# A router's constants moved into a planned instruction list, with other estimates for clears, and five deferred operations moved ahead of a loop

## The chip, the core and the metric

The kernel runs on one core of a Trainium2 chip. The metric is device time in microseconds (us) of one execution; the time shown is a median of runs. TensorE (PE) multiplies matrices, VectorE (DVE) and ScalarE (ACT) work elementwise, GpSimd (POOL) makes indices and issues indirect DMAs, and SyncE (SP) issues the other DMAs. Each engine works through its own instructions in order and waits for others at semaphores.

## What is computed

A recurrence over 768 steps for 32 heads of width 40, then a mixture of experts with one expert for each of 3072 tokens, then a dense MLP:

```python
for t in range(S):                                    # recurrence
    y[:, :, t] = np.einsum('bhd,bhde->bhe', rt, state)
    Sa = np.einsum('bhde,bhe->bhd', state, at)
    state = state * wt[:, :, None, :] - np.einsum('bhd,bhe->bhde', Sa, bt) \
            + np.einsum('bhd,bhe->bhde', vt, kt)
x = y.transpose(0, 2, 1, 3).reshape(3072, 320)
logits = x @ w_gate + modality_bias[modality_id]      # router, 8 experts
e_idx = np.argmax(logits, axis=1)
gate_w = softmax(logits)[np.arange(N), e_idx]
for e in range(8):                                    # first MLP: 320 -> 1024 -> 320
    out[mask] = gate_w[mask, None] * (np.maximum(x[mask] @ w1[e], 0.0) @ w2[e])
h = out @ w_in                                        # second MLP: 320 -> 2048 -> 320
return (h * (1.0 / (1.0 + np.exp(-1.702 * h)))) @ w_out
```

## The kernel before

Operands of matmuls are split into two fp16 parts, high and low, whose products are added in PSUM.

**The recurrence** (class Attn) goes in 24 chunks of 32 steps. Work that doesn't depend on the state is done ahead: the decays (clamped on DVE, then two scans and transposes), the triangular solves, the products of keys and values. The state S is carried from chunk to chunk in two halves (the DVE instruction "S<-s,P", 46 of them). After each chunk a row of 128 tokens goes through the router: `row` scales and splits it, PE multiplies by the gate, and for groups of up to four chunks `route` picks the expert and scatters the tokens to DRAM (POOL's indirect DMAs "XD<-XR,desti"). Near the end the first experts' weights are fetched ("raw<-in_W,w0row") and the first slots of the first MLP are computed.

All of this is written down as a list of operations (class Plan), not issued at once. `emit` estimates the length of each operation (`cost`), runs nine rounds of a forward and a backward list schedule over the engines, and issues the instructions in the order of the best round; on the chip each engine then takes them in that order. Some operations may go to either of two engines (`either`, with the engine chosen by the planner): the clears of large zeroed tiles (`clear`: gbd, tbd, nbd, xbd, zbd, kb, pick), the roundings of masked products (mg), the placings of blocks in the zeroed tiles (gbd, tbd, xbd, zbd), and others. In the profile nearly all of this has line L250, which is that of the issuing helper.

The router's constants (identity and triangle masks, index tables made by POOL's iota and cast on DVE, gate weights split in two parts, the bias by modality) are made by `consts`, ahead of the list and outside it, in program order. Their temporaries have a pool of their own. In the list a clear on DVE is estimated by

```python
if op == "memset":
    return 10 + n * (0.85 if eng == "gpsimd" else 0.26 if half else 1.04)
```

**The first MLP** (`moe1`) goes through slots of 128 tokens in order of experts. Beside it the weights of the second MLP are loaded as 64-bit numbers, put together from words on DVE (tiles wt and f, lines L1113 to L1119) and split (OH on ACT, OL on DVE, lines L1141 and L1142). What is left of that at the end is a generator, `self.rest`, whose pieces are taken one at a time by `next(self.rest, None)`: four at the end of `moe1`, then one in each round of the second MLP's loop but the round k = 1.

**The second MLP** (`moe2`) runs through 96 steps, each a block of 512 tokens by 128 hidden columns: `up` on PE, `gate` (t on DVE, sigmoid on ACT), `high` (g on DVE, gh on ACT), `low` (gl on DVE), and three steps later `down` (acc on PE). In this part a scheduler of the framework keeps nearly the order of the program.

Of the kernel before, what the change touches and what calls it, by code (L numbers as in the profile page):

```python
# [14 lines left out]
class Pool:  # L15


    def __init__(self, pool, bufs):
        self.pool, self.bufs, self.tiles, self.turn = pool, bufs, {}, {}
# [26 lines left out]
class Given:  # L46
# [5 lines left out]
    def tile(self, shape, dt, tag=None, name=None):  # L52
        ts = self.tiles[tag or name]
        ts.append(ts.pop(0))
        assert list(ts[-1].shape) == list(shape) and ts[-1].dtype == dt, tag
        return ts[-1]


class Carve:
# [23 lines left out]
class Plan:  # L83
# [117 lines left out]
    def cost(self, eng, op, a, k):  # L201
        aps = [p for x in list(a) + list(k.values()) for p in self.aps(x)]
        out = k["out"] if "out" in k else a[0]
        n = max(self.size(p) for p in aps)
        psum = any("PSUM" in str(getattr(p.tensor, "_space", "")) for p in aps)
        half = all(p.dtype == mybir.dt.float16 for p in aps if self.size(p) > 1)
        if eng == "tensor":
            m = self.size(out)
            wide = k["lhsT"].dtype != mybir.dt.float16 if op == "matmul" else True
            return max(m * (2 if wide else 1) / PEHZ + (2.5 if PEHZ > 2 else 0), 20.0 if op == "matmul" and self.size(k["lhsT"]) <= 32 else 25.0)  # L210
        if eng == "scalar":
            return ((51 if psum else 93) + n / 1.2 + (190 if "accum_out" in k else 0)
                    + (94 if isinstance(k.get("scale"), bass.AP) else 0))
        if op == "indirect_dma_start":
            return 1040.0
        if op == "memset":
            return 10 + n * (0.85 if eng == "gpsimd" else 0.26 if half else 1.04)
        if op == "affine_select":
            return 130 + n
        if eng == "gpsimd":  # L220
            return 147 + (1.888 if out.dtype == mybir.dt.float16 else 2.1) * n
        if eng == "sync":
            if op == "dma_start":
                return 475.0 if k["out"].ap[0][1] == 128 else 650.0
            return 1180.0 if n <= 512 else 1245.0 if n <= 1024 else 2140.0
        if op == "reciprocal":
            return 69 + 6.2 * n
        if op == "tensor_tensor_scan":
            return 2.13 * n
        if op == "transpose":  # L230
            return 1.9 * n
        if op == "tensor_tensor" and max(len(p.ap) for p in aps) > 4:
            return 69 + 1.75 * n
        rate = 1.0
        if op == "tensor_copy" and not psum:
            rate = 0.25 if half else 0.5
        elif op == "tensor_scalar" and not psum:
            rate = 0.35 if half else 0.5
        return 69 + n / 0.96 * rate
# [276 lines left out]
class Mlp:  # L516
# [4 lines left out]

    def consts(self, w_gate, modality, bias):
        tc, ctx = self.tc, self.ctx
        p = self.cp = ctx.enter_context(tc.tile_pool(name="mconst", bufs=1))
        with tc.tile_pool(name="mtemp", bufs=1) as tp:
            self.consts_in(p, tp, w_gate, modality, bias)

    def consts_in(self, p, tp, w_gate, modality, bias):
        nc = self.nc
        self.id16 = p.tile([128, 128], F16, name="id16")  # L530
        self.idb = p.tile([128, 128], mybir.dt.bfloat16, name="idb")
# [45 lines left out]
        m = tp.tile([128, NTILE], mybir.dt.int64, name="mod")  # L577
# [392 lines left out]
    def next(self, xp):  # L970

        self.xtile = lambda: xp.tile([128, XROW], F32, tag="xg", name="xg")

    def moe1(self, fill, flags):
# [3 lines left out]
        with tc.tile_pool(name="m1", bufs=2, side="right", reuse_waits="tile") as p, \  # L978
# [81 lines left out]
            self.rest = fill[2]()  # L1060
            fill[0](NFIX - 1)
            down(NFIX - 1, to=last)
            for _ in range(4):
                next(self.rest, None)

    def slots(self, fit, p, ps):

# [197 lines left out]
    def moe2(self, out):  # L1265
# [5 lines left out]
        with ExitStack() as c2, \  # L1271
# [47 lines left out]
            def done(b, c):  # L1319
# [6 lines left out]
                if b == NB - 1:  # L1326
# [4 lines left out]
                sent.append(nc.gpsimd.indirect_dma_start(  # L1331
                    out=out, out_offset=bass.IndirectOffsetOnAxis(ap=X["ti"][:, c:c + 1], axis=0), in_=o, in_offset=None))

            for k in range(N + LOOK):
                n = k - LOOK
                b, f = steps[n] if n >= 0 else (0, -1)
                if f == 0 and b + 1 < NB:
                    self.gather2(b + 1)
                if k < N:
                    up(k)  # L1340
                if 0 <= k - 2 < N:
                    low(k - 2)
                if k < N:
                    gate(k)
                if 0 <= k - 1 < N:
                    high(k - 1)
                if k != 1:
                    next(self.rest, None)
                if 3 <= f <= 10 and b + 1 < NB:
                    self.ready2(b + 1, f - 3, bank)  # L1350
                if 0 <= n < N - LATE:
                    for c in range(4):
                        down(n, c)
                        if f == NF - 1:
                            done(b, c)
# [636 lines left out]
def body(tc, A, out):  # L1992
    nc = tc.nc
    with ExitStack() as ctx:
# [9 lines left out]
        with ExitStack() as c1:  # L2004
            pool = lambda n, b: c1.enter_context(tc.tile_pool(name=n, bufs=b, side="right", reuse_waits="tile"))
            lent = m.weights1(pool("m1w", 1), A["W1"], A["W2"])
            with ExitStack() as c2:
                p = Pool(c2.enter_context(tc.tile_pool(name="rt", bufs=1)), 1)
                ps = Pool(c2.enter_context(tc.tile_pool(name="rps", bufs=1, space=PSUM)), 1)
                at = Attn(tc, c2, A["WU"], A["AB"], A["KVR"], kp, lent)  # L2010
                plan = m.nc = at.plan
                plan.between = m.between
                Y, sent, read, later = {}, [], [], []

# [86 lines left out]
```

## Time and profile before

| | us |
|---|---|
| median of 3 runs | 1054.72 (1052.9 to 1058.57) |
| the profiled execution | 1058.96, its span 1057.2 |
| PE, DVE, ACT, POOL busy in the span | 896.7, 847.4, 688.6, 134.9 |
| recurrence: first to last state instruction | 70.66 to 510.25 |
| PE's first product of an expert | 537.12 |
| PE's first product of the second MLP | 723.75 |

Rows of a timeline give start and length of an instruction, or of a run of like ones (x count), and in brackets the idle time of the engine before it with what ended it. SPq rows are issues of DMAs. In tables by stretch, the busy time of each engine stands with its number of instructions.

### The profile page before, as it was taken

How to read it: one execution, taken by the hardware profiler on the slowest of the kernel's cores; microseconds unless marked ns; L12 is line 12 of the kernel's file. 1: busy time of each engine (PE TensorE's matmuls, PEld its weight loads, DVE VectorE, ACT ScalarE, POOL GpSimd, SP SyncE). 2: the span in 40 equal slices, each digit the busy share in tenths (PEclk: the TensorE clock that was granted, in tenths of full speed). 3: DMA queues.
4: the chain of work that ended last, by engine and by line, in shares of the span. 5: the costliest groups of instructions: out<-in, count | busy, mean ns of one | idle time of the engine just before them, and what ended most of it. 6: DMA issues, size and time to landing. Idle time of an engine off the chain costs nothing. (4 is left out here: it accounts for less than half of the span.)

```text
span 1057.2 us, 36944 instructions
## 1 busy us (share of the span) xinstructions
PE 896.7 (85%) x15558; PEld 661.3 (63%) x15558; DVE 847.4 (80%) x2074; ACT 688.6 (65%) x1498; POOL 134.9 (13%) x221
## 2 busy tenths in 40 slices
PE   0168787678789788787879999999999999999996
PEld 0147666567667567666768888885555555555554
DVE  8998999899999899997865778778866666666654
ACT  4568899799899899997753356455444434443432
POOL 2000000020020020010234113302021111212000
PEclk9999799787566786878979999999999999999999
DMA  3659879789977968976737689763011111111100
GB/s 106 143 134 176 155 143 176 155 151 162 185 174 166 170 157 155 185 116 92 152 121 250 102 231 271 183 139 91 14 38 38 33 38 31 44 32 45 25 20 29
DMA packets 249306, 127.64 MB, mean 121 GB/s; under 512 B 232800, under 2 KB 236640, under 8 KB 248096
## 3 DMA queue, kind: packets, MB, share of 16 engines
q1 hardware_dynamic: 243456, 98.10, 48.9%
q0 software_dynamic: 5664, 27.01, 8.0%
q8 instruction: 124, 2.03, 0.8%
q14 instruction: 62, 0.51, 0.2%
HBM read 56.21 MB, written 12.16 MB: 65 GB/s over the span
## 5 line engine op out<-in xcount | busy, mean ns | idle before, releaser
L1298 ACT ACTIVATE sg<-t 128x512 f32<-128x512 f32 x96 | 60.5, 630 | 178.7 <-DVE t L1296 178.7
L1292 PE MATMUL h<-xT,WH 128*128 128x512 f16 x480 | 119.3, 379 | 0.0
L1316 PE MATMUL acc<-OH,gh 128*128 128x320 f16 x384 | 114.8, 299 | 1.4 <-ACT gh L1304 1.4
L1316 PE MATMUL acc<-OH,gl 128*128 128x320 f16 x384 | 114.8, 299 | 0.3 <-DVE gl L1308 0.3
L1316 PE MATMUL acc<-OL,gh 128*128 128x320 f16 x384 | 114.8, 299 | 0.0
L1316 PEld LDWEIGHTS <-gh 128*128 128x128 f16 x768 | 74.9, 98 | 44.5 <-ACT gh L1304 1.9
L1308 DVE TENSOR_TENSOR gl<-g,gh 128x512 f16<-128x512 f32 x96 | 66.2, 690 | 40.8 <-ACT gh L1304 40.6
L1296 DVE TENSOR_TENSOR t<-h,sB 128x512 f32<-128x512 f32 x96 | 66.1, 688 | 39.5 <-PE h L1292 39.5
L250 POOL DMA_INDIRECT XD<-XR,desti x24 | 31.0, 1290 | 471.6 <-ACT TT L250 206.7
L923 PEld LDWEIGHTS <-split 128*128 128x128 f16 x1472 | 84.0, 98 | 2.7 <-ACTq L987 1.1
L923 PE MATMUL h<-xT,split 128*128 128x128 f16 x1408 | 82.8, 219 | 0.8 <-ACTq L987 0.8
L1292 PE MATMUL h<-xT,WL 128*128 128x512 f16 x288 | 77.8, 379 | 0.0
L948 PE MATMUL y<-split,hh 128*128 128x320 f16 x352 | 75.3, 299 | 0.2 <-issue 0.2
L1292 PEld LDWEIGHTS <-WH 128*128 128x128 f16 x480 | 47.0, 98 | 41.8
L250 PE MATMUL w<-s,pick 128*128 128x160 f16 x368 | 64.0, 288 | 8.3 <-DVE s L250 2.7
L250 PEld LDWEIGHTS <-kb 64*128 64x128 f16 x2208 | 47.3, 100 | 37.7 <-issue 24.2
L250 PEld LDWEIGHTS <-tbd 128*128 128x128 f16 x1152 | 51.3, 104 | 23.2 <-issue 10.5
L1302 DVE SCALAR_TENSOR_TENSOR g<-h,sg 128x512 f32<-128x512 f32 x96 | 65.2, 680 | 0.0
L1304 ACT CAST gh<-g 128x512 f16<-128x512 f32 x96 | 59.3, 618 | 1.7 <-DVE g L1302 1.4
L937 DVE SCALAR_TENSOR_TENSOR hl<-h,hh 128x512 f16<-128x512 f32 x46 | 30.3, 686 | 28.0 <-ACT hh L936 23.3
L948 PE MATMUL y<-split,hl 128*128 128x320 f16 x176 | 52.6, 299 | 0.0
L1331 POOL DMA_INDIRECT out<-o,ti x20 | 22.0, 1101 | 227.3 <-ACT o L1325 224.5
(362 smaller groups left out, 2396.7 us busy)
## 6 DMA issues: line engine op xcount, KB each, us to landing
K<-in_KVR SPq DMA_DIRECT2D x24, 480.0 KB, 4.8
raw<-in_AB SPq DMA_DIRECT2D x13, 640.0 KB, 4.2
s<-in_wi SPq DMA_DIRECT2D x12, 512.0 KB, 6.9
s<-in_wo SPq DMA_DIRECT2D x10, 512.0 KB, 4.5
raw<-in_WU SPq DMA_DIRECT2D x6, 660.0 KB, 4.1
YS<-ys SPq DMA_DIRECT2D x23, 160.5 KB, 2.5
Sd<-s SPq DMA_TRANSPOSE x46, 4.3
out<-o SPq DMA_DIRECT2D x4, 160.0 KB, 3.4
```

What stands on the lines that cost most here:

```text
L250: r = self.made[i] = getattr(getattr(self.nc, e), op)(*a, **k)
L923: nc.tensor.matmul(h[:, f4, :], lhsT=a, rhs=b, start=(j == 0), stop=(j == 7))
L937: nc.vector.scalar_tensor_tensor(hl[:, s, :], h, 0.0, hh[:, s, :], op0=ALU.max, op1=ALU.subtract)
L948: nc.tensor.matmul(y, lhsT=a[:, f, :], rhs=V(b, f), start=(n == 0), stop=(n == 23))
L1292: nc.tensor.matmul(h3, lhsT=a, rhs=r, start=(j == 0), stop=(j == 7))
L1296: nc.vector.tensor_tensor(t, hs[k], self.xs[steps[k][0]]["sB"], op=ALU.mult)
L1298: nc.scalar.activation(sgs[k], t, AF.Sigmoid, scale=1.702)
L1302: nc.vector.scalar_tensor_tensor(gs[k], hs.pop(k), 2.0 ** -4, sgs.pop(k), op0=ALU.mult, op1=ALU.mult)
L1304: nc.scalar.copy(ghs[k], gs[k])
L1308: nc.vector.tensor_tensor(gls[k], gs.pop(k), ghs[k], op=ALU.subtract)
L1316: nc.tensor.matmul(accs[c], lhsT=a[:, s], rhs=r[:, f, :], start=(f == 0 and j == 0), stop=(f == NF - 1 and j == 2))
L1331: sent.append(nc.gpsimd.indirect_dma_start(out=out, out_offset=bass.IndirectOffsetOnAxis(ap=X["ti"][:, c:c + 1], axis=0), in_=o, in_offset ...
```

## The change

- The router's constants are no longer made ahead of the list: `consts` keeps a function, and it is called once the list exists, so that their instructions stand in the list and are placed by the planner. Their temporaries are cut from tiles that the recurrence lends (class Lent).
- The planner estimates a clear as 20 ns and 0.43 or 0.89 ns an element on DVE, in place of 10 ns and 0.26 or 1.04.
- Of the deferred pieces, the four at the end of `moe1` go away and five are taken ahead of the loop of `moe2`; the loop takes none in the rounds k = 0 and k = 1.

```diff
+class Lent:
+    def __init__(self, lend):
+        self.lend = lend
+    def tile(self, shape, dt, name=None):
...
+        t = self.lend(-(-n * mybir.dt.size(dt) // 8) * 2).bitcast(dt)[:, 0:n]
...
         if op == "memset":
-            return 10 + n * (0.85 if eng == "gpsimd" else 0.26 if half else 1.04)
+            return 20 + n * (0.85 if eng == "gpsimd" else 0.43 if half else 0.89)
...
-        p = self.cp = ctx.enter_context(tc.tile_pool(name="mconst", bufs=1))
-        with tc.tile_pool(name="mtemp", bufs=1) as tp:
-            self.consts_in(p, tp, w_gate, modality, bias)
-
-    def consts_in(self, p, tp, w_gate, modality, bias):
+        self.cp = ctx.enter_context(tc.tile_pool(name="mconst", bufs=1))
+        self.consts_in = lambda tp: self.fixed(self.cp, tp, w_gate, modality, bias)
+
+    def fixed(self, p, tp, w_gate, modality, bias):
...
             down(NFIX - 1, to=last)
-            for _ in range(4):
-                next(self.rest, None)
...
+            for _ in range(5):
+                next(self.rest, None)
             for k in range(N + LOOK):
...
-                if k != 1:
+                if k > 1:
                     next(self.rest, None)
...
                 plan = m.nc = at.plan
+                m.consts_in(Lent(lent))
                 plan.between = m.between
```

How the order of the instructions changes is shown at three places. The first is the start of DVE, up to the clamp of the decays ("raw_152<-raw_151" before, "raw_71<-raw_70" now: both are parts of the tiles raw1 and raw2, cut into buffers) and the first scan. The names if, key, mf and biast are the router's constants, sel, neg and pos those of the recurrence. Before:

```order
36 L250 MEMSET gbd 128x1024
37 L551 CAST if_79<-io_77 128x32
40 L557 TENSOR_SCALAR key<-if_79 128x32
44 L569 TENSOR_SCALAR if_103<-if_103 32x24 x3
45 L250 TENSOR_TENSOR sel<-sel,s_198 128x64
48 L250 MEMSET tbd 128x1024
49 L250 MEMSET kb 128x2048
54 L250 TENSOR_SCALAR pos_226<-pos_226 128x128
59 L250 TENSOR_SCALAR pos<-pos 128x128
61 L250 MEMSET xbd 128x1024
62 L250 TENSOR_SCALAR raw_152<-raw_151 128x40x32
63 L250 SCALAR_TENSOR_TENSOR raw_151<-raw_152,one 128x1320
```

The clamp is DVE's row 62. Now it is row 28, and the rows ahead of it are the recurrence's own:

```order
11 L266 MEMSET split_72 128x1024
12 L266 MEMSET one 128x40
21 L266 MEMSET kb 128x2048
22 L266 TENSOR_TENSOR sel<-sel,s_117 128x64
23 L266 MEMSET tbd 128x1024
24 L266 TENSOR_SCALAR neg_142<-neg_142 128x128
27 L266 TENSOR_SCALAR pos_145<-pos_145 128x128
28 L266 TENSOR_SCALAR raw_71<-raw_70 128x40x32
29 L266 SCALAR_TENSOR_TENSOR raw_70<-raw_71,one 128x1320
```

The clears of gbd and xbd have left DVE; the router's casts are DVE's rows 181 to 193 now. The second place is the start of ACT. Before:

```order
2 L250 ACTIVATE one<-on 128x1320
3 L250 ACTIVATE nbd<-on 128x2048
4 L250 ACTIVATE pick<-on 128x512
5 L250 ACTIVATE zbd<-on 128x2048
6 L250 ACTIVATE raw_152,viol<-raw_151,wb 128x40x32
10 L250 ACTIVATE pb<-raw_151,par 128x40 x2
11 L250 ACTIVATE P_236<-y_235 128x64
12 L250 ACTIVATE ast<-raw_151 128x16x80
```

Now ACT clears two more tiles ("<-on" are clears; pb and P are the decays' products over a chunk, ast the first stack of operands):

```order
2 L266 ACTIVATE one<-on 128x1320
3 L266 ACTIVATE gbd<-on 128x2048
4 L266 ACTIVATE nbd<-on 128x2048
5 L266 ACTIVATE pick<-on 128x512
6 L266 ACTIVATE raw_71,viol<-raw_70,wb 128x40x32
10 L266 ACTIVATE pb<-raw_70,par 128x40 x2
11 L266 ACTIVATE xbd<-on 128x2048
12 L266 ACTIVATE P_183<-y_182 128x64
13 L266 ACTIVATE zbd<-on 128x2048
14 L266 ACTIVATE ast<-raw_70 128x16x80
```

gbd's clear has taken the place of zbd's ahead of row 6, and xbd's and zbd's stand between pb and ast. The third place is DVE at the seam between the two MLPs. Before:

```order
1609 L1142 SCALAR_TENSOR_TENSOR OL<-f,OH 128x512
1610 L1113 TENSOR_SCALAR wt<-s 128x512
1611 L1115 SCALAR_TENSOR_TENSOR wt<-s,wt 128x512
1612 L1296 TENSOR_TENSOR t<-h,sB 128x512
1613 L1117 SCALAR_TENSOR_TENSOR f<-s,wt 128x512
1614 L1119 SCALAR_TENSOR_TENSOR f<-ab,f 128x512
1615 L1142 SCALAR_TENSOR_TENSOR OL<-f,OH 128x512
1616 L1296 TENSOR_TENSOR t<-h,sB 128x512
1617 L1302 SCALAR_TENSOR_TENSOR g<-h,sg 128x512
1618 L1308 TENSOR_TENSOR gl<-g,gh 128x512
```

Now the deferred pieces stand ahead of the first gate:

```order
1609 L1155 SCALAR_TENSOR_TENSOR OL<-f,OH 128x512
1610 L1126 TENSOR_SCALAR wt<-s 128x512
1611 L1128 SCALAR_TENSOR_TENSOR wt<-s,wt 128x512
1612 L1130 SCALAR_TENSOR_TENSOR f<-s,wt 128x512
1613 L1132 SCALAR_TENSOR_TENSOR f<-ab,f 128x512
1614 L1155 SCALAR_TENSOR_TENSOR OL<-f,OH 128x512
1615 L1309 TENSOR_TENSOR t<-h,sB 128x512 x2
1616 L1315 SCALAR_TENSOR_TENSOR g<-h,sg 128x512
1617 L1321 TENSOR_TENSOR gl<-g,gh 128x512
```

The first t has moved behind two more pieces and an OL; the rows from g on are the same.

## Rows read from the trace of the kernel before

**Rows 1.** The chain that ended last, its first long piece (start, length, what).

```profile
719.26 0.69 DVE OL L1142
```

**Rows 2.** Busy time by stretch (stretch, length, then each engine; then clock and DMA).

```profile
0.00:15.14 15.14, 0.00 (x0) 0.00 (x0) 10.34 (x68) 10.75 (x11) 5.85 (x34) 1.00 0.26 81
15.14:70.66 55.52, 11.48 (x361) 9.04 (x365) 54.74 (x88) 24.92 (x51) 0.00 (x0) 1.00 0.57 140
70.66:449.36 378.70, 309.75 (x8959) 248.97 (x8956) 353.57 (x959) 346.14 (x816) 21.05 (x24) 0.78 0.90 164
449.36:510.25 60.89, 49.22 (x1422) 40.75 (x1419) 51.98 (x175) 48.64 (x125) 4.65 (x8) 0.83 0.73 110
...
537.12:723.75 186.63, 184.99 (x2370) 159.59 (x2370) 138.47 (x312) 95.94 (x181) 49.39 (x73) 0.99 0.72 184
...
732.92:1057.20 324.28, 316.35 (x1906) 185.58 (x1906) 212.11 (x376) 138.64 (x260) 42.56 (x61) 1.00 0.12 32
```

**Rows 3.** The first stretch, DVE's instructions of the list alone (line L250).

```profile
0.00:15.14 15.14, 7.49 (x43) 1.00 0.26 81
```

**Rows 4.** DVE at the start (start, length, instruction, idle before it).

```profile
0.90 0.17 DVE L534 MEMSET ones<- 128x128 f16 x1 [0.90 <-PEq L2091]
...
3.27 0.91 DVE L250 MEMSET split<- 128x1024 f32 x1 [0.26 <-issue]
...
6.21 0.91 DVE L250 MEMSET gbd<- 128x1024 uint32 x1 [0.16 <-issue]
...
10.06 0.23 DVE L250 TENSOR_TENSOR sel<-sel,s 128x64 f32<-128x64 f32 x1 [1.86 <-POOL s L250]
...
11.84 1.76 DVE L250 MEMSET kb<- 128x2048 uint32 x1 [0.38 <-issue]
...
15.14 0.76 DVE L250 TENSOR_SCALAR raw<-raw 128x1280 f32<-128x1280 f32 x1
```

**Rows 5.** ACT at the start: one clear, and two waits.

```profile
5.62 1.89 ACT L250 ACTIVATE zbd<-on 128x2048 f16<-128x2048 f16 x1
...
18.88 0.62 ACT L250 ACTIVATE pb<-raw,par 128x40 f32<-128x40 f32 x2 [7.16 <-DVE raw L250]
...
26.37 1.29 ACT L250 ACTIVATE ast<-raw 128x1280 f16<-128x1280 f32 x1 [5.88 <-DVE raw L250]
```

**Rows 6.** The decays' first load: its issue, and such loads' time to landing.

```profile
2.19 0.43 SPq L250 DMA_DIRECT2D raw<-in_WU  x1
...
raw<-in_WU SPq DMA_DIRECT2D x2, 660.0 KB, 3.9
```

**Rows 7.** Groups by form, 0 to 545 us (busy us, mean ns, idle before).

```profile
L250 ACT ACTIVATE tbd<-TT,own 128x512 f16<-128x512 f16 x43 | 30.2, 721 | 0.1
...
L250 DVE TENSOR_SCALAR tbd<-TT,own 128x512 f16<-128x512 f16 x53 | 16.8, 347 | 0.0
...
L250 ACT CAST mgG<-mx 128x256 f16<-128x256 f32 x17 | 6.9, 407 | 7.0 <-DVE mx L250 7.0
...
L250 DVE CAST mgG<-mx 128x256 f16<-128x256 f32 x7 | 2.0, 287 | 0.0
```

**Rows 8.** DVE's state instructions, the first and the last of 46.

```profile
70.66 0.49 DVE L250 TENSOR_TENSOR S<-s,P 128x320 f32<-128x320 f32 x1 [0.19 <-PE s L250]
...
510.25 0.48 DVE L250 TENSOR_TENSOR S<-s,P 128x320 f32<-128x320 f32 x1
```

**Rows 9.** The first fetch of expert weights, and PE's first product with them.

```profile
522.74 0.98 POOL L250 DMA_INDIRECT raw<-in_W,w0row  x1 [0.19 <-issue]
...
537.12 1.44 PE L250 MATMUL w<-aE,split 128*128 128x128 f16 x12 [3.30 <-ACT aE L250]
```

**Rows 10.** The seam between the two MLPs, on ACT, DVE and PE.

```profile
724.50 0.62 ACT L1141 ACTIVATE OH<-f 128x512 f16<-128x512 f32 x1
...
726.83 0.68 DVE L1296 TENSOR_TENSOR t<-h,sB 128x512 f32<-128x512 f32 x1
...
732.92 0.31 PE L1316 MATMUL acc<-OH,gl 128*128 128x320 f16 x1 [0.28 <-DVE gl L1308]
```

More of the change, by code (lines that the diff above doesn't have):

```diff
@@ L56, in tile @@
         return ts[-1]
+class Lent:
+    def __init__(self, lend):
+        self.lend = lend
+    def tile(self, shape, dt, name=None):
+        n = 1
+        for d in shape[1:]:
+            n *= d
+        t = self.lend(-(-n * mybir.dt.size(dt) // 8) * 2).bitcast(dt)[:, 0:n]
+        if len(shape) == 2:
+            return t
+        names = "abc"[:len(shape) - 1]
+        return t.rearrange(f"p ({' '.join(names)}) -> p {' '.join(names)}", **dict(zip(names, shape[1:])))
 class Carve:
```

## The prediction

> **What bounds the kernel now.** I read the chain first, then the busy time by stretches, then the start and the two seams row by row. The chain that ended last can be followed back only to 719.26 us [rows 1] and is nearly all TensorE of the second MLP, so the stages are read one by one. From 537.12 to 723.75 us PE is busy 184.99 of 186.63 us, and from 732.92 us to the end 316.35 of 324.28 [rows 2]: both MLPs are set by PE, and whatever comes before 537 us moves the end one for one. In the recurrence it is otherwise. From 70.66 to 449.36 us DVE is busy 353.57 and ACT 346.14 of 378.70 us, PE 309.75: two engines are nearly full and share out the work. From 449.36 to 510.25 us DVE falls to 51.98 of 60.89 and ACT to 48.64. Before 15.14 us DVE is busy only 10.34 us, and from there to 70.66 us ACT has only 24.92 of 55.52. The change works at this start and at the seam at 724 us.
>
> **The start, removed.** The first real work of the recurrence on DVE is the clamp of the decays at 15.14 us [rows 4]. Up to it DVE is busy 10.34 us and idle 4.80. Of the busy time 7.49 us belong to the list's own instructions [rows 3], the other 2.85 us to the router's constants, which the new order has behind the clamp. So has it five small clears and one scaling of pos: of those 43 instructions five are the long clears (4 x 0.91 + 1.76 = 5.4 us [rows 4]), the other 38 come to 0.055 us each, and six of them to 0.3 us. The clears of gbd and xbd, 0.91 us each, are ACT's now. That leaves 7.49 - 0.3 - 1.8 = 5.4 us of work ahead of the clamp. The idle time that stays is 0.90 us before the first instruction and the short waits ahead of the three long clears that stay (0.26 us split, 0.38 us kb, and 0.16 us for tbd as for gbd): 1.7 us. The wait of 1.86 us ahead of sel goes, since POOL, whose queue had held a copy back for the router's casts, makes sel's parts first. The clamp starts near 5.4 + 1.7 = 7.1 us, 8.0 us earlier. The decays' load stands first on SP now; it was issued at 2.19 us and takes 3.9 us to land [rows 6], and so would land near 5 us, before the clamp asks for it. ACT comes to its first Relu of the decays behind the same three clears and pick as before, gbd's in zbd's place, so at the time of before; it is not what the clamp waits for.
>
> **The start, coming back.** Of the 8.0 us, 1.8 us are clears that ACT does and 4.80 - 1.7 = 3.1 us are idle time. The rest, 3.1 us, is work that still has to be done: the router's constants, which now stand between rows of the first chunks, and the small clears. ACT makes xbd's and zbd's clears between pb and ast, 1.89 us each [rows 5]. It sits idle for 7.16 us ahead of pb and for 5.88 us between pb and ast, so 3.8 us fit and cost nothing; were that cover gone, they would cost 3.8 us. The Trainium skill's page "Trainium Architecture — The Big Picture", in "The five engines, in one table", says that ScalarE is not for simple arithmetic and that per element VectorE is up to about three times faster. The rows agree in kind, 1.89 us on ACT against 0.91 on DVE for one clear; by the rule alone moving two would lose about 2 us of engine time and leave 2.7 us of the sum below, while the idle rows put it at nothing.
>
> **Choices that fall otherwise.** The new estimates redraw the whole list. Counted over it, 13 roundings of the masked products (mg) go from ACT to DVE, 13 x 0.287 = 3.7 us on DVE and 13 x 0.407 = 5.3 us off ACT [rows 7]; six placings of tbd go the other way, 6 x 0.347 = 2.1 us off DVE and 6 x 0.721 = 4.3 us onto ACT. The other moved choices go both ways and I put them at nothing. Net 1.6 us more on DVE, 1.0 us less on ACT.
>
> **What reaches the end.** If DVE alone decided the recurrence, 8.0 - 3.1 - 1.6 = 3.3 us would be left. If the chain of states decided it (the S rows, 46 of them, from 70.66 to 510.25 us, two to a chunk, so 439.6 / 45 x 2 = 19.5 us a chunk [rows 8]), the returned work would fall into idle time and all 8.0 us would stay. DVE idles 378.70 - 353.57 = 25.1 us in the long stretch and 8.9 us in the 60.89 us that follow, where the returned 4.7 us can partly sink. I take 4.5 us, nearer to the DVE's end, because DVE is the fullest engine. Behind the last S row nothing changes in kind: the first fetch of expert weights goes out at 522.74 us, behind four scatters on POOL, and PE's first expert product comes at 537.12 us [rows 9]. POOL's order there is the same in both kernels, so the shift is handed on whole, and PE carries it through the first MLP.
>
> **The seam at 724 us.** The five deferred operations are the same in number up to the loop's first round, only all ahead of it. DVE's first gate, t, ran at 726.83 us [rows 10], three rows ahead of an OL; now it follows that OL, as the second t does. ACT's OH of 724.50 us, for which the first OL waits, stood behind a copy of ys and now stands ahead of it; I estimate half a us for that. The first t costs 0.3 us of it, since DVE now makes it behind the second OL and not while it would wait for OH. So gl, which PE's first acc waits for at 732.92 us, comes 0.2 us earlier. Neither end is far: 1 us late if OH does not start earlier and t pushes everything by its own 0.68 us, 1 us early if the second t is done before the sigmoid is asked for. The copy of ys goes out later, and what is stored from it is gathered only blocks later.
>
> **Sum.** -4.5 - 0.2 = -4.7 us. The profiled execution took 1058.96 us (1057.2 us of span and 1.8 us around it), so it would take 1054.3. The median of the runs shown is 1054.72 us, 4.2 us less than the profiled one, and the same gain on it gives 1050.0 us.
>
> **Rivals.**
> 1. The chain keeps everything: 8.0 + 0.2 = 8.2 us, 1046.5 us. For it: 7 to 9% of idle time on the two engines in the long stretch and 15 to 20% in the last one [rows 2]. Against it: the constants stand between rows of chunks whose DVE hardly rests. Chance 0.25.
> 2. The start gives little: the redrawn list waits 3 to 6 us more in its 500 us than the old one, and the time stays at 1052 to 1056, say 1054. For it: each of some 1,250 DVE rows can change its neighbours. Against it: the tail of the list is nearly row for row the same. Chance 0.20.
> 3. Slower. The 13 roundings that DVE takes over stand between the mask row (mx) and the difference (mg), in the line that every chunk's state waits for, and behind other DVE rows instead of on the less full ACT. Each of the 22 distances between S rows then grows. From 4.7 / 22 = 0.21 us per chunk the gain is gone; at 0.5 us it is 11 - 4.7 = 6.3 us slower, 1061 us. Against it: DVE's rounding takes 0.287 us where ACT's takes 0.407 us, so each is also shorter. Chance 0.10.
>
> The forecast, 1047.5 to 1052 us, has the other 0.45.
>
> **How the numbers follow.** Half a per cent (5.3 us) is about what a measurement of this kernel can tell from no change, so faster begins below 1049.4 us. Faster: rival 1 and some two fifths of the forecast, 0.25 + 0.17 = 0.42. Slower: rival 3, 0.10. Same: the rest, 0.48. The range from 1043.5 to 1056.5 us takes in all of the forecast, most of rivals 1 and 2 and the 1 us of the seam; outside are rival 3 and the ends of the others.
>
> **What would show it.** The clamp's row near 7.1 us instead of 15.14, and no wait for POOL ahead of sel. ACT's xbd and zbd clears inside its idle time before ast. The first S row near 63 us, the router's casts among the rows of the first three chunks, and the last S row near 505.5 us. The first fetch near 518 us and PE's first expert product near 532.5 us. At the seam, PE's idle time ahead of acc unchanged within 1 us. Wrong it would be if the distance between S rows differs from 19.5 us a chunk by more than 0.2, or if the clamp waits for the load or for ACT.

## The result, and the profile after

The changed kernel takes 1065.98 us (median of 11 runs, 1058.5 to 1072.11) where the kernel before takes 1058.57 (11 runs on the same chip, the three shown above among them): ratio 1.0077, 95% interval 1.0052 to 1.0103. That is 7.4 us slower, where 4.7 us faster was forecast. The forecast's base of 1054.72 was the median of three runs; eleven give 1058.57, so 3.9 us of its miss in absolute time lie in the base. The profiled execution is the slowest of the 11: 1072.11 us, span 1070.4, 13.1 us over the span before; what follows takes these 13.1 us apart, and not the 7.4 us of the medians. Executions of one kernel spread by up to 20 us, and those over 1.5% above their kernel's fastest are left out of the ratios; one profile below (the changed kernel's on chip D) comes from such an execution and is used only to see where a stall stands.

The stretches of the changed kernel, as in [rows 2] (stretch, length, then PE, PEld, DVE, ACT and POOL busy; clock, DMA share, GB/s), cut at the clamp, the first, ninth and last state row, PE's first product of an expert, and the seam:

```profile
0.00:7.33 7.33, 0.00 (x0) 0.00 (x0) 5.08 (x36) 6.52 (x5) 5.23 (x24) 1.00 0.49 165
7.33:63.59 56.26, 11.93 (x389) 9.95 (x390) 55.16 (x95) 32.65 (x60) 4.68 (x8) 1.00 0.59 137
63.59:143.58 79.99, 60.04 (x1793) 48.61 (x1790) 68.78 (x201) 63.70 (x151) 1.52 (x4) 0.82 0.99 153
143.58:510.89 367.31, 289.71 (x8529) 236.34 (x8529) 340.19 (x962) 330.34 (x781) 24.75 (x32) 0.78 0.91 155
510.89:545.95 35.06, 17.23 (x547) 14.61 (x547) 20.70 (x93) 20.02 (x51) 10.48 (x19) 0.78 0.65 114
545.95:734.71 188.76, 185.19 (x2369) 159.56 (x2369) 139.11 (x314) 96.18 (x181) 51.31 (x73) 0.99 0.72 182
743.50:1070.39 326.89, 316.35 (x1906) 185.57 (x1906) 212.27 (x376) 138.64 (x260) 42.62 (x61) 0.99 0.13 31
```

The kernel before, the same view, from its first to its ninth and from its ninth to its last state row:

```profile
70.66:142.92 72.26, 60.54 (x1794) 48.32 (x1791) 66.19 (x185) 63.77 (x153) 0.00 (x0) 0.88 0.95 162
142.92:510.25 367.33, 298.44 (x8587) 241.40 (x8583) 339.35 (x949) 331.01 (x788) 25.69 (x32) 0.76 0.86 156
```

The early start is there: the clamp stands 7.8 us earlier and the first state row 7.1 us. Four chunks later nothing is left of it. The ninth state row stands at 143.58 us against 142.92, and from there to the last one both kernels take 367.3 us in these two profiles. (That they agree so closely is partly chance: further down, two profiles of one order on one chip differ by some 4 us in this stretch, 372.1 and 375.8 on C, 374.4 and 378.2 on E.) In these four chunks DVE has 2.6 us more work (68.78 against 66.19) and 5.1 us more idle time (11.2 against 6.1). DVE on the changed kernel, the rows that answer to [rows 4] and [rows 8], and the one wait of interest:

```profile
5.92 0.16 DVE L266 TENSOR_TENSOR sel<-sel,s 128x64 f32<-128x64 f32 x1
...
7.33 0.82 DVE L266 TENSOR_SCALAR raw<-raw 128x1280 f32<-128x1280 f32 x1
...
63.59 0.48 DVE L266 TENSOR_TENSOR S<-s,P 128x320 f32<-128x320 f32 x1
...
100.13 0.49 DVE L266 TENSOR_TENSOR K<-K,F 128x320 f32<-128x320 f32 x1 [2.94 <-DMA K<-in_KVR]
...
143.58 0.49 DVE L266 TENSOR_TENSOR S<-s,P 128x320 f32<-128x320 f32 x1 [0.32 <-PE s L266]
...
510.89 0.49 DVE L266 TENSOR_TENSOR S<-s,P 128x320 f32<-128x320 f32 x1
```

DVE's waits between the first and the ninth state row (what waited, for what: us in all, times, longest), first of the changed kernel:

```profile
DVE K L266 <- DMA K<-in_KVR: 6.4, 3, 2.9
DVE mx L266 <- PE g L266: 1.5, 1, 1.5
DVE ast L266 <- DMA aE<-ast: 1.3, 1, 1.3
```

and of the kernel before:

```profile
DVE K L250 <- DMA K<-in_KVR: 2.7, 1, 2.7
DVE mx L250 <- PE g L250: 2.5, 4, 1.0
```

Loads of K and one transpose cost 5.0 us more, which is about the added idle time. K, the tile with a chunk's k, v and r, has one buffer. Its last reader ended at 87.9 us (rst, 0.48 us from 87.42), but on SP the next load stood behind four transposes (UE, Sd, vE and kE are transposed operands for PE):

```profile
87.24 2.12 SPq L266 DMA_TRANSPOSE UE<-ust  x1
89.46 1.27 SPq L266 DMA_TRANSPOSE Sd<-s  x1
90.89 1.23 SPq L266 DMA_TRANSPOSE vE<-vst  x1
92.21 2.24 SPq L266 DMA_TRANSPOSE kE<-kst  x1
94.50 0.58 SPq L266 DMA_DIRECT2D K<-in_KVR  x1
```

It was issued 6.6 us after the buffer was free. The DMA share of this stretch is 0.99.

Behind the last state row there is a second loss. From it to PE's first expert product it is 35.06 us against 26.87 [rows 8, 9]. The fetch goes out at nearly the old distance, but the gathers behind it on POOL wait for the scatters ahead of it, and the last of the fetch's 128 packets ends 16.9 us behind its issue, before 9.4:

```profile
523.83 0.98 POOL L266 DMA_INDIRECT raw<-in_W,w0row  x1 [0.19 <-DVE XR L266]
...
535.66 0.97 POOL L266 DMA_INDIRECT xg<-XD,xrow  x1 [10.37 <-DMA XD<-XR,desti]
...
545.95 1.33 PE L266 MATMUL w<-aE,split 128*128 128x128 f16 x11 [2.21 <-ACT aE L266]
```

The seam, as in [rows 10], went as forecast: from PE's first product of the second MLP to the first acc 8.79 us, before 9.17.

```profile
734.75 0.63 ACT L1154 ACTIVATE OH<-f 128x512 f16<-128x512 f32 x1 [2.69 <-DVE f L1132]
739.99 1.28 DVE L1309 TENSOR_TENSOR t<-h,sB 128x512 f32<-128x512 f32 x2
743.50 0.31 PE L1329 MATMUL acc<-OH,gl 128*128 128x320 f16 x1 [0.28 <-DVE gl L1321]
```

Last, the span ends 10.5 us behind PE's last product; before it was 8.0. So the 13.1 us between the two profiles are: 0.6 us at the last state row (7.1 won, 7.7 lost), 8.2 us up to the first expert product, 2.1 us in the first MLP (whose cause was not looked for; PE's work there is the same within 0.2 us), -0.4 us at the seam, 0 in the second MLP, 2.6 us at the end of the program.

### The profile page after: what moved, and what is told of

Same layout as the page of the kernel before. It is cut to its first block, busy times and chain, and to the rows that moved or that the text cites. A ratio compares the mean times of both kernels' runs of the same rounds, so it can differ in the third digit from the quotient of the medians.

```text
span 1070.4 us, 36942 instructions
## 1 busy us (share of the span) xinstructions
PE 888.0 (83%) x15558; PEld 657.8 (61%) x15558; DVE 847.7 (79%) x2082; ACT 692.1 (65%) x1490; POOL 141.1 (13%) x221
## 5 line engine op out<-in xcount | busy, mean ns | idle before, releaser
L1305 PE MATMUL h<-xT,WL 128*128 128x512 f16 x288 | 77.8, 379 | 0.0
L266 PE MATMUL w<-s,pick 128*128 128x160 f16 x368 | 57.8, 274 | 10.6 <-ACT Ss L266 6.1
L266 PE MATMUL s<-vst,kb 64*128 64x54 f16 x1104 | 36.5, 200 | 19.8 <-ACT kb L266 18.2
```

Of the source, the lines that this page charges most:

```text
L266: r = self.made[i] = getattr(getattr(self.nc, e), op)(*a, **k)
L1305: nc.tensor.matmul(h3, lhsT=a, rhs=r, start=(j == 0), stop=(j == 7))
```

## Experiments

Each ratio is to runs of the kernel before taken beside it, with its 95% interval; the runs fell on four chips, named B to E; the one above is called A. Stages are from one profile each. The kernel before took 1084 us on B, C and E, 1057 on D.

**The change in its parts, chip B.** The changed kernel as it is:

> The changed kernel once more. Theory A (the weight fetch at the end of the recurrence meets the transposes of Sd and UE in every run of this order): from the last S row to PE's first expert product again 33 to 37 us (35.1 in the first profile, 26.9 before), last S row within 2 us of 510.9, ratio to before 1.005 to 1.010. Theory B (the packets of up to 11 us near 525 us were an accident of that execution, and the loss sits in the recurrence, where the returned work and new waits ate the 7 us of the start): 26 to 29 us for that stretch, last S row again near 510 us, span nearer 1061, ratio 1.002 to 1.008.

The deferred pieces alone (`for _ in range(5): next(self.rest, None)` ahead of the loop, none at the end of `moe1`):

> The kernel before with only the five deferred pieces moved ahead of the second MLP's loop. Theories A and B both: PE's first product of the second MLP to its first acc with gl takes 8.8 us instead of 9.2, the time within 0.3% of before. A rival (the seam hides a loss in the loop): ratio over 1.004.

The estimates alone:

```diff
-            return 10 + n * (0.85 if eng == "gpsimd" else 0.26 if half else 1.04)
+            return 20 + n * (0.85 if eng == "gpsimd" else 0.43 if half else 0.89)
```

> The kernel before with only the new estimates for clears. The list is redrawn and gbd and xbd are cleared on ACT, the router's constants stay ahead. The clamp then starts near 13.3 us (15.1 less 1.8). If the redrawn order is what loses: last S row at 510 to 515 us and ratio 1.002 to 1.010. If the constants' place is what loses: last S row near 508.5 us, ratio 0.997 to 1.000.

The constants in the list alone (`m.consts_in(Lent(lent))`, old estimates, old places of the deferred pieces):

> The kernel before with only the router's constants in the list, old estimates. The clamp starts near 10.5 us. If the constants between the rows of the first chunks are what loses: the S rows fall back by 4 us or more over the first ten and the last S row is at 509 us or later, ratio 1.002 to 1.010. If the estimates lose: last S row at 506 to 509 us, ratio 0.994 to 1.000. Theory A would show the long way from the last S row to PE's first expert product only if fetch and transposes stand as close in time as in the changed kernel.

Measured, us from the profiles (with the kernel before on A for comparison):

| | first S | first to last S | last S to first expert product | seam | behind last product | ratio |
|---|---|---|---|---|---|---|
| before, A | 70.66 | 439.6 | 26.9 | 9.18 | 8.0 | |
| changed, A | 63.59 | 447.3 | 35.1 | 8.79 | 10.5 | 1.0077 (1.0052 to 1.0103) |
| changed, B | 63.59 | 456.4 | 36.3 | 8.78 | 10.5 | 1.0004 (0.9978 to 1.0030) |
| deferred alone, B | 70.47 | 450.6 | 35.6 | 8.79 | 8.2 | 0.9995 (0.9968 to 1.0022) |
| estimates alone, B | 69.76 | 447.8 | 31.2 | 9.18 | 7.8 | 0.9988 (0.9962 to 1.0014) |
| constants alone, B | 66.48 | 458.0 | 38.6 | 9.18 | 8.1 | 1.0052 (1.0028 to 1.0077) |

On chip B the changed kernel is as fast as the one before, so neither theory A nor theory B has it right. The 35 us behind the last state row, thought of as the new order's, is there with the old order too (deferred alone keeps it). By the ratios the constants alone lose half a per cent and the estimates alone nothing. The first to the last state row is longest where the constants stand in the list: from the first to the ninth row DVE has 69.98 us of work there, 65.56 with the estimates alone and 66.13 in the old order. The ninth state row stands at 142.8 us (deferred alone), 143.3 (changed), 144.6 and 143.5, from first rows between 63.6 and 70.5: as if something held it there.

**Does the start count at all? Chip C.** The order of the changed kernel untouched, and fillers on DVE alone:

```diff
+                if i == self.clamp:
+                    self.nc.vector.memset(self.spin, 1.0)
+                    for _ in range(9):
+                        self.nc.vector.reciprocal(self.spin, self.spin)
                 self.issue(i, e)
```

> The changed kernel with its instruction order untouched, and 10 idle-time fillers put on DVE alone (a clear and nine reciprocals of a 128x128 scratch tile, about 7.9 us together) just ahead of the clamp of the decays, so that the clamp comes at 15.2 us as in the kernel before; ACT, POOL and SP start early as in the changed kernel. In both profiles of the changed kernel the first state row stands at 63.6 us and the ninth at 143.3 to 143.6; in both profiles of the old order at 70.5 to 70.7 and 142.8 to 142.9. Theory P (the first four chunks are held by something other than DVE's start, above all by the loads of K and the transposes, whose DMA engines are full from 60 to 120 us): first state row at 71.5 us, ninth at 143.5 to 147, and the end no more than 3 us later than that of the changed kernel. Theory O (the start counts one for one, and the new order of the instructions spends 7 us more in the first four chunks): first state row 71.5, ninth 151.2 to 151.6, last row and end 7.9 us later.

```profile
7.59 8.85 DVE L304 RECIPROCAL split<-split 128x128 f32<-128x128 f32 x9
16.36 0.76 DVE L266 TENSOR_SCALAR raw<-raw 128x1280 f32<-128x1280 f32 x1
...
72.50 0.48 DVE L266 TENSOR_TENSOR S<-s,P 128x320 f32<-128x320 f32 x1
...
152.45 0.49 DVE L266 TENSOR_TENSOR S<-s,P 128x320 f32<-128x320 f32 x1 [0.31 <-PE s L266]
```

Ratio 1.0079 (1.0043 to 1.0115). The fillers took 9.0 us, not 7.9; the first row moved by 8.9 and the ninth by 9.1 to 10.1 (from 143.31 on B, 142.38 in the next kernel on C). Theory P is out: nothing holds the ninth row, the start counts one for one, and it is the new order that spends more on the four chunks. It does so on other chips too: from the first to the ninth row 80.0 us against 72.3 in the old order on A, 79.7 against 72.3 on B, 77.8 against 71.7 on E, and 79.9 here with the fillers.

**The end of the program, chip C.** Six small loads more on SP (they run at 580 to 586 us, early in the first MLP and not beside its end):

```diff
+        for i in range(6):
+            nc.sync.dma_start(out=spare[:, i], in_=A["wg"])
         rv = nc.values_load(m.usual[0:1, 0:1], min_val=0, max_val=1)
```

> The changed kernel with six small loads more on SP (12 KB each, of the gate weights, into a scratch tile, beside the end of the first MLP), whose only purpose is that SP's last instructions stand elsewhere in its stream. In the changed kernel the span ends 10.5 us behind the last product on PE in both profiles, and 7.8 to 8.2 us behind it in the four kernels with other instruction streams; in the changed kernel SP takes one wait, then nothing for 2.05 us while an 8 KB packet of the instruction queue passes, then the rest. Theory C (a boundary between two loads of code lies among SP's last waits): 8.0 to 8.5 us behind the last product, and the whole 2 us shorter than the changed kernel. Rival (the stores land later in the changed kernel, or its last instructions differ): 10.5 us again. All else as in the changed kernel, first state row 63.6, ninth 143.5.

Ratio 0.9979 (0.9957 to 1.0000); the span ends 7.9 us behind the last product. The DMA traffic of the last 6 us in 40 slices, first of the changed kernel, then of this one:

```profile
GB/s 17 0 0 9 17 9 9 26 0 0 0 0 0 0 0 55 0 0 0 0 0 0 0 0 0 0 0 0 0 55 0 0 0 0 0 0 0 0 0 0
```

```profile
GB/s 296 127 339 364 271 51 68 421 330 296 159 25 0 0 0 8 63 17 8 17 8 0 0 0 0 0 0 0 54 0 0 0 0 0 0 0 0 0 0 0
```

A slice is 0.15 us, and the first one lies 4.5 us behind PE's last product in the changed kernel, 1.9 us in this one. In the changed kernel the stores are done at 1.2 us, then come two single packets of 8192 B of the instruction queue 2.2 us apart, and only then the end. SP takes one of its last waits 6.24 us behind the last product and the next at 8.29 us, with the first of these packets at 6.80 between them. With six loads more the stores run until 3 us, one such packet is left behind them, and SP's last waits follow each other without such a gap. Over all profiles of this study, the six with the changed kernel's unpadded SP row have 9.3 to 10.5 us here, the twelve others 7.3 to 8.2. So 2 us of the loss have to do with a packet of code among SP's last waits, and with no work of the kernel.

**The loads of K, chip C.** On SP each load directly behind its buffer's last reader; no other engine's order changes:

```diff
+        for x in [x for x in order if x[1] in self.soon and self.preds[x[1]]]:
+            order.remove(x)
+            last = max(k for k, y in enumerate(order) if y[1] in self.preds[x[1]])
+            order.insert(last + 1, x)
```

> The changed kernel with one edit to its order: on SP each load of K stands directly behind the last instruction, of any engine, that reads the buffer it fills, in place of the planner's place behind one to three transposes; no other engine's order changes. In the changed kernel DVE waits 6.4 us for loads of K between the first and the ninth state row (2.7 us in the old order), and they were issued up to 6.6 us after the buffer was free. Theory P1 (these loads, late on SP, hold the first four chunks): DVE's wait for K there falls to 2 us or less, the ninth state row comes at 139 to 141 in place of 143.5, and the end 3 to 4 us earlier. Rival P2 (the DMA engines are full, so that what one load gains a transpose loses): the wait for K falls, a wait for transposed tiles (aE, kE, rE, UE) on PE grows by the same, ninth row at 143 to 144, end the same. Theory O (the order of DVE's own rows decides): ninth row at 142.5 to 143.5, end the same within 1.5 us.

The wait for K fell to 3.1 us (P1 had 2 or less; the padded kernel has 4.1), the ninth row came at 139.83, within P1's 139 to 141; but the end was not 3 to 4 us earlier: the last row stands at 520.0 and the ratio is 1.0037 (1.0017 to 1.0057), slower. Against the padded kernel on the same chip it is 2.6 us ahead at the ninth row, 3.5 at the thirteenth, 1.3 behind at the twenty-first and 5.5 behind at the last. P1 is right for the four chunks. That it is the later loads, moved in the same way, that cost more than they bring was not tested one by one.

**The change without its first part, chip C** (estimates and deferred pieces; constants ahead of the list):

> The change without its first part: the router's constants stay ahead of the list, with the new estimates of clears and the five deferred pieces ahead of the second MLP's loop. If putting the constants in the list is what costs the stretch from the first to the last state row its 6 to 8 us, this kernel has the clamp at 12.8, the first state row at 69.8, some 3 us less than the changed kernel from first to last, 0.4 us less at the seam than before, 8.2 us behind the last product, and comes out 0.1 to 0.4 per cent faster than the kernel before. If the constants' place makes no difference to the sum, it is within 0.1 per cent of the kernel before.

Clamp 12.68, first row 69.66, ninth 141.79, last 518.74; ratio 0.9997 (0.9968 to 1.0026). No change, as for the two parts alone; the interval takes in most of the 0.1 to 0.4 per cent that were expected, so it doesn't decide between the two readings.

**The early loads for the chunks 1 to 6 only (`if c <= 6`), with the padding, chip D:**

> The changed kernel with both earlier edits, the second one cut short: six small loads more on SP beside the end of the first MLP, and only the loads of K for the chunks 1 to 6 directly behind the last reader of their buffer. Theory: the earlier loads win 2.5 to 3.5 us up to the ninth state row (139 to 140 in place of 142.4 to 143.6), which the full edit kept up to the thirteenth row and lost where later loads were moved; so here the last state row also comes some 3 us sooner than in the padded kernel, and the time is 0.4 to 0.6 per cent under the kernel before. Rival: what is won ahead of the ninth row is lost again behind it whatever the order there (the planner's later order is drawn for the old times): ninth row at 139 to 140, last row no sooner, 0.1 to 0.3 per cent under the kernel before.

```profile
90.54 0.52 SPq L266 DMA_DIRECT2D K<-in_KVR  x1
...
97.47 0.49 DVE L266 TENSOR_TENSOR K<-K,F 128x320 f32<-128x320 f32 x1 [0.57 <-DMA K<-in_KVR]
...
137.60 0.49 DVE L266 TENSOR_TENSOR S<-s,P 128x320 f32<-128x320 f32 x1
...
504.91 0.49 DVE L266 TENSOR_TENSOR S<-s,P 128x320 f32<-128x320 f32 x1 [0.16 <-PE s L266]
```

From the first to the ninth state row, as in the tables by stretch above:

```profile
64.07:137.60 73.53, 58.97 (x1794) 47.20 (x1790) 68.21 (x202) 63.32 (x150) 1.53 (x4) 0.86 1.01 159
```

DVE's idle time there is 5.3 us, in place of 11.2 in the changed kernel and 6.1 in the one before; its work stays 2 us above that of the kernel before. K's load is issued 4 us earlier, DVE waits 0.57 us in place of 2.94 there, the ninth row stands at 137.60, and from it to the last it is 367.31 us, as in both profiles on A: here the gain is kept to the last row. Yet the ratio is 1.0030 (0.9995 to 1.0066), neither of the two that were expected; the runs fall into two groups, 1054 to 1061 and 1064 to 1072.

**The changed kernel and the one before on chip D:**

> The changed kernel once more. It came out at 1.0077 of the kernel before on one chip and at 1.0004 on another. If the difference is one of chips (the stretch between the last state row and the first product of an expert was 8 us shorter for the kernel before on the first chip, 26.9 against 35.1, and the same for both orders on the second, 35.6 and 36.3), then the ratio is near 1.000 wherever the kernel before has 35 us there, and near 1.008 where it has 27 us. If it is not, the ratio falls between, whatever that stretch. 2.1 to 2.5 us of it belong to the end of the program.

> The kernel before, for its profile on this chip beside the changed kernel's: first state row at 70.5, ninth at 142.8, 8 us behind the last product; from the last state row to the first product of an expert 27 us if that belongs to its order of instructions, 35 to 36 us if it belongs to the chip.

Ratio 1.0033 (0.9991 to 1.0076), between the two expected. The changed kernel's twelve runs there fall into two groups, five at 1053.8 to 1059.1 us and seven at 1066.4 to 1074.0, where the 29 runs of the kernel before lie between 1051.4 and 1067.0; its profile is of one of the seven. What parts the groups is not shown: a profile of one of the five was not taken. From the last state row to the first expert product the kernel before has 26.9 us as on A, the changed one 32.0, with the same stall behind the fetch as on A; here the rows of the changed kernel on D,

```profile
527.83 0.98 POOL L266 DMA_INDIRECT raw<-in_W,w0row  x1 [0.19 <-DVE XR L266]
...
538.18 0.98 POOL L266 DMA_INDIRECT xg<-XD,xrow  x1 [8.97 <-DMA XD<-XR,desti]
```

and those of the kernel with the six early loads there, which has the same rows on POOL:

```profile
517.82 0.98 POOL L266 DMA_INDIRECT raw<-in_W,w0row  x1 [0.19 <-issue]
...
521.95 0.98 POOL L266 DMA_INDIRECT xg<-XD,xrow  x1 [2.42 <-DVE XR L266]
```

In the stalled profiles 14 (A) and 5 (D) of the fetch's packets of 12288 B took over 3 us, the longest 11.4 and 8.7; in the other four profiles on A and D the longest took 2.9.

**Old order with the early loads, chip D** (the kernel of constants ahead, estimates and deferred pieces):

> The router's constants ahead of the list as before, the new estimates, the five deferred pieces ahead of the loop, and the loads of K for the chunks 1 to 6 directly behind the last reader of their buffer. Without the last edit the first state row stands at 69.7, the ninth at 141.8 with 3.5 us of waiting of DVE for K, the last at 518.7, and the ratio is 0.9997. Theory: DVE's wait for K falls to 1.5 us or less, ninth row at 139.5 to 140.5, last row 2 us sooner, 0.2 per cent under the kernel before or better. Rival: the DMA engines are full there, another transposed tile is late for it, ninth row at 141 to 142 and no change at the end.

It failed: DVE's wait for K 4.0 us, ninth row 144.62, last 516.47, ratio 1.0066 (1.0034 to 1.0098), slower than before. The same edit that wins some 3 us up to the ninth row in one order wins nothing in another.

**The fetch behind the last transposes, chip E** (on the kernel with padding and six early loads; on POOL a copy of a column of UE ahead of the fetch, and both behind UE's transpose in the list):

> The padded kernel with the early loads of K, and the first fetch of expert weights moved on POOL behind the landing of the last chunk's transposed UE (by a copy of one column of UE on POOL ahead of the fetch); everything behind it on POOL, four gathers of tokens and the second fetch, moves with it. Both profiles of the changed kernel on the faster chips had up to 15 packets of the first fetch, 12288 B each, that took 8.7 to 11.4 us, a wait of 9.0 to 10.4 us on POOL for the scatters ahead of it, and 32 to 35 us from the last state row to the first product of an expert, while four other profiles there had 26 to 27 and no packet over 2.9 us. Theory T (the fetch and the last transposes, issued within 0.3 us of each other, block each other in some executions): no packet of the fetch over 4 us, the fetch 3 to 5 us later, the stretch 28 to 31 us in its profile, and the runs of this kernel spread less (the slowest within 10 us of the fastest). Rival (the stall has to do with the scatters or with chance, not with the transposes): runs spread as before (15 to 20 us), or the stretch is 32 us and more. On a chip where the stretch is 35 us for every order, nothing can be told but the fetch's packets.

> The padded kernel with the early loads of K for the chunks 1 to 6, once more, beside the kernel with the fetch moved. Its first twelve runs came out at 1.0030 of the kernel before, between 0.9995 and 1.0066, and fell into two groups, eight at 1054 to 1061 us and four at 1064 to 1072; its profile was from the faster group, with the ninth state row at 137.6 and the last at 504.9. If the early loads hold on any chip: ninth row at 137 to 140, and the time 0.2 to 0.5 per cent under the kernel before where the stall at the fetch does not show.

> The changed kernel, for its profile on this chip. If the stall of the first fetch belongs to this order of instructions on a fast chip: packets of 12288 B over 8 us again, POOL waiting 9 us or more for the scatters, 32 to 35 us from the last state row to the first product of an expert. If it comes by chance: a profile without it is as likely as one with it. On a slower chip 36 us without such packets.

> The kernel before, for its profile on this chip: 27 us from the last state row to the first product of an expert and no packet of the fetch over 3 us on a fast chip, 35 to 36 us on a slower one; ninth state row at 142.8 to 143.0.

E is of B's kind: the kernel before has 36.8 us behind the last state row, the changed one 34.4, and no packet of the fetch over 2.1 us. So for the stall nothing can be told, as was said beforehand for such a chip. The fetch went out 9.0 us later, counted from the last state row, not 3 to 5. What the run does show is the other side: where the fetch goes out first, the transposes on SP are held up. SP's last transposes with the fetch ahead of them (the padded kernel, chip C) and with it behind (chip E; the same kernel without this edit has 5.49 and 6.14 us on E):

```profile
529.47 5.38 SPq L266 DMA_TRANSPOSE Sd<-s  x2
535.01 6.27 SPq L266 DMA_TRANSPOSE UE<-ust  x1
```

```profile
528.75 2.59 SPq L266 DMA_TRANSPOSE Sd<-s  x2
531.51 1.23 SPq L266 DMA_TRANSPOSE UE<-ust  x1
```

The Trainium skill's page "Trainium Kernel Development and Optimization", under "Key Constraints", says that DMAs of SP, ACT and POOL all run on the same 16 DMA engines and interleave. These rows agree: with POOL's fetch 6 us ahead of it, UE's issue on SP takes five times as long as without. It depends on how far behind: over all profiles, a transpose that SP issued up to 1.2 us behind the fetch took 1.23 to 1.29 us (so UE's on A and D, in the stalled profiles too), and one issued 1.4 to 8 us behind it 1.7 to 8.2 us (only on B, C and E, where SP comes to them later). The stretch is no shorter for the edit (35.8 us against 36.4; the weights come 8.5 us later), and the ratio is 0.9957 (0.9935 to 0.9979), beside 0.9974 (0.9954 to 0.9993) for the kernel without this edit. Both are a little faster than the kernel before, and the two intervals overlap; against the changed kernel the second is not told apart (1.0004, 0.9978 to 1.0030, on B). The ninth row stands at 139.3 with the edit and 140.4 without, in the changed kernel at 141.3.

## Why the prediction was wrong

- **The start, removed.** Right. Clamp 7.33 (7.1 forecast; DVE 5.08 us busy and 2.25 idle ahead of it, 5.4 and 1.7 forecast), no wait for POOL ahead of sel, first state row 63.59 (near 63). ACT makes gbd's, xbd's and zbd's clears with 3.0 us idle left ahead of ast.
- **The start, coming back.** The amount was near: DVE has 3.4 us more work between first and last state row (408.97 against 405.55), where 4.7 were reckoned (3.1 returned, 1.6 choices).
- **What reaches the end** is the step that failed. 4.5 us were to stay, because the returned work could partly sink into DVE's 25 us of idle time. From first to last row the loss is 7.7 us on A (5.7 on B against the deferred pieces alone, 8.6 on E), so nothing stays: the last row comes 0.6 us late. Idle time did not take the work in, it grew by 4.3 us. The share of idle time was taken as a store to be filled; but those gaps were waits for others. In the four chunks where the work came back, the new order lets loads of K stand behind transposes on SP. With the loads moved forward the account closes: DVE's idle time is back at 5.3 to 7.7 us in the four kernels with early loads (old order 5.6 to 6.4, changed order 9.0 to 11.2), and what stays is about the 2.6 us of more work, none of it sunk (four chunks 73.5 to 76.3 us against 71.7 to 72.4).
- **Rival 2** names half of the mechanism (the redrawn list waits more) and was given 0.20; its size, 3 to 6 us, was near (5.1 us more idle time on A up to the ninth row). Not foreseen was its place: not scattered over 500 us, but on A all within the first four chunks, so that the first loads on SP were the rows to look at. The late-start run confirms the start's worth, the early loads take most of the added waits away again (ninth row on average 142.6 us in the five profiles of the changed kernel's order, 139.3 in the four with early loads).
- **Rival 3** shows nowhere: from the ninth row on both orders take 367.3 us on A, with 13 roundings moved; on B the changed order takes 1.7 us less than the old one, on E 2.5 us more, within the scatter of some 4 us. **Rival 1** is out with what failed.
- **The shift handed on whole behind the last row.** Wrong on A: 8.2 us more up to the first expert product, the largest part of the 13.1 us and a second term that was put at nothing. Why the fetch stalls is not settled. How close the fetch and UE's transpose are issued doesn't settle it: 0.2 us apart in both stalled profiles, but in the kernel before on A both go out at 522.74 us, without a stall. It was seen in both profiles of the changed kernel on chips where the stretch can be 27 us, in none of four profiles of other kernels there, and one of these four has the same rows on POOL; the padded order without it is therefore possible. On B, C and E all orders have 31 to 39 us, and the changed kernel's ratio on B is 1.0004.
- **The seam.** Right: -0.39 us (-0.2 forecast), in every kernel with the deferred pieces ahead.
- **Not in the sum:** 2 us at the end of the program, from a packet of code among SP's last waits.

## What to carry to other kernels

Idle time of an engine in a stretch is room for more work only if one knows what it waits for; here the gaps stayed when the work was added, and the work came on top. When a planner's list is redrawn, compare first the order on the queue that feeds the stretch, here SP's, and not only the engines that compute. A gain of the size of the planner's scatter needs several draws or a fixed order with one edit, as in the runs that left the list alone and moved one kind of row.

## What the runs showed of the hardware

- Chips differ by kind: the kernel before takes 1057 to 1059 us on A and D and 1084 on B, C and E (each chip was measured in one sitting, so chip and hour are not told apart). The second MLP from its first acc on takes 316.4 us on all of them. The difference lies in the stages ahead of it: first to last state row (old order) 436 to 440 against 447 to 451, the stretch behind it 27 against 36 to 37, the first MLP 186 to 187 against 192 to 194.
- In the stretch behind the last state row PE on chip E has pauses for which the profile shows no releaser, and none of these on D (the kernel before, PE's longest waits, E then D):

```profile
PE y L250 <- issue: 3.9, 8, 0.5
PE g L250 <- DMA UE<-ust: 3.1, 1, 3.1
```

```profile
PE g L250 <- DMA UE<-ust: 2.2, 1, 2.2
PE r L250 <- ACT XR L250: 1.6, 1, 1.6
```

- A packet of 8192 B of the instruction queue behind the last store costs about 2 us at the end of the span; six more loads on SP, issued some 490 us earlier, took it away.
